# From output 1000 on: convolutions with 13 products per 4 outputs, end terms added onto sums that VectorE seeds in PSUM

## The chip, the cores and the metric

One core of a Trainium2 chip. The metric is the device time of one execution in microseconds (us); lower is better. Times are medians of several executions. On one core an execution counts as slow when it is over 1.5% above the fastest of the same kernel.

Engine names in the profile: PE = TensorE (matmuls), DVE = VectorE, ACT = ScalarE, POOL = GpSimd, SP = SyncE (here: DMA issue).

## The reference, cut to what matters

```python
B, T, D, K, U = 2, 4000, 512, 5, 8
h = gelu(conv5(x, w1))[:, ::2, :]      # 5 taps, zero padding, every second output: 2000 rows per b
f = gelu(conv5(h, w2))[:, ::2, :]      # the same again: 1000 rows per b
fe = f @ w_f;  ge = g @ w_g
j = tanh(fe[:, :, None, :] + ge[:, None, :, :])
out = j @ w_o                          # [2, 1000, 8, 512], bf16
```

So there are two convolutions of stride 2, then a large "joint" product of 16000 rows. The change is to the convolutions. "Output 1000" means row 1000 of `h` for b = 0; the products before it stay as they were, but with tiles of 252 and 248 columns instead of 254 and 246. The joint product is the same, but the PSUM banks that it rotates over are not.

Each kernel's output agreed with the reference within tolerance, but that comparison cannot see the convolutions. Worked out from the reference's inputs on a host, dropping the whole convolution path changes the outputs by less than 1e-6, against a largest output of 2.6e-4. So the runs show times. They do not show that the 13-product arithmetic is right, nor that the end products really accumulate onto what VectorE wrote into PSUM.

## The kernel before: the parts the argument touches

A stride-2 convolution of 5 taps splits into 3 even and 2 odd taps. For 2 outputs at a time, 7 filtered products do the work of 10 direct ones. Each product needs a transformed input (sums and differences of input phases) and a transformed weight.

A tile has 500 column pairs, so each matmul has 500 columns; only the first 1000 outputs are cut into two tiles, t0 and t1, with matmuls of 254 and 246 columns, so that work can start early. One tile is 4 output blocks (`m`) x 7 products x 4 contraction blocks = 112 matmuls.

```python
def xf(src, off, dst, c0, n, which, keep=False):        # VectorE: one transform, 4*n elements
    ...
    elif which == "a1":
        tt("dve", o(1), ph(0), ph(2), add)
    elif which == "a2":
        tt("dve", ph(2), ph(2), ph(0), sub)

def wsum04(wsb, wt, eng, m):                            # GpSimd: weight sums of layer 2
    sl = slice(m * P, (m + 1) * P)
    tt(eng, ssum[:], wsb[0, :, sl], wsb[4, :, sl], add)
    tt(eng, wt[0, :, sl], ssum[:], wsb[2, :, sl], sub)
    tt(eng, wsb[2, :, sl], ssum[:], wsb[2, :, sl], add)

def post(self, m, where, vec=(), scal=(), first=()):    # output transform of one block
    A, C, Dd, step = where
    act(c, ps.cols(C, n), ACT.Copy, scale=0.5)
    ...
    for s, f in ((0, 0.5), (1, -0.5)):                  # VectorE: one input in PSUM
        # t[s] = f * PSUM[Dd] + c
        ...
    for f in vec:                                       # transforms of the next tile
        f()
    tt("dve", tv, tv, ps.pair(A, step, n), add)         # VectorE: SBUF + PSUM
    pending.append(lambda: self.gelu(m, tv))

# entering: the first tiles
t1.xf("a0"); w1sums(0, "s"); w1sums(0, "+"); t1.xf("b1"); t1.xf("b3")
t1.xf("a1"); w1sums(0, "-"); t1.xf("a2"); t1.shift("a3"); t1.xf("a3")
post0(1); post0(2, ...); post0(3)
...
if qi == 3:                                             # late: GpSimd makes layer 2's sums
    wsum13(w2_sb, w2_t, "pool", m * P, (m + 1) * P)
    wsum04(w2_sb, w2_t, "pool", m)
```

Here `tt(engine, out, a, b, op)` is one elementwise operation on two inputs. The layer-1 weight sums are made by VectorE at the start. GpSimd has only small set-up operations until it makes the layer-2 sums from 56 us on. TensorE never needs a result of VectorE *inside* a block: it fills PSUM, and VectorE reads it afterwards.

## Time and profile before

| | before |
|---|---|
| time, median of the first 3 executions | 278.26 us (278.15 to 278.85) |
| span of the profiled execution, granted TensorE clock | 276.5 us, 1.000 |
| TensorE, VectorE, GpSimd busy | 98%, 68%, 11% |
| last matmul group of t1 done, next tile begins | 33.42 us |
| joint product begins | 158.63 us |

The page of the kernel before. The first line after the span has the busy us of each engine, with the share of the span and the number of instructions. The rows after it cut the span into 40 equal slices; each digit is the busy share in tenths (PEclk: the granted clock). The last lines are the chain of work that ended last, by engine.

```profile
span 276.5 us, 3847 instructions
...
PE 271.3 (98%) x1422; PEld 136.7 (49%) x1422; DVE 188.9 (68%) x249; ACT 163.0 (59%) x194; POOL 30.9 (11%) x38
...
PE   8899999999999999999999999999999999999995
...
DVE  2899997977966785775433374766766766766764
...
POOL 1000000079995000000000000000000000000000
PEclk9999999999999999999999999999999999999999
...
PE 96%; DMA 2%; SPq 0%; ACT 0%; issue 0%
```

The chain is TensorE almost alone: a matmul saved anywhere would be time saved. But an average of 68% hides that VectorE is full in slices 3 to 6 (14 to 41 us), exactly where the change adds work.

Lines of the timeline of the kernel before (start us, duration us, engine, line of the program, operation, output<-inputs, shape, count of equal instructions joined):

```profile
22.53 0.67 DVE L287 TENSOR_TENSOR xs<-xs 128x984 bf16<-128x984 bf16 x1
23.11 0.67 DVE L287 TENSOR_TENSOR xt<-xt,xs 128x984 bf16<-128x984 bf16 x1
...
23.66 0.59 PE L298 MATMUL acc<-xs,w_t 128*128 128x246 bf16 x4
24.09 0.58 PE L298 MATMUL acc<-xt,w_sb 128*128 128x246 bf16 x4
...
27.83 1.19 DVE L287 TENSOR_TENSOR xt<-xt,xs 128x2000 bf16<-128x2000 bf16 x1
...
66.49 1.16 POOL L287 TENSOR_TENSOR ssum<-w_sb 128x512 f32<-128x512 bf16 x1
...
66.85 3.93 DVE L287 TENSOR_TENSOR xt<-xt,xs 128x2000 bf16<-128x2000 bf16 x2
70.70 1.18 DVE L287 TENSOR_TENSOR ty<-ty,acc 128x1000 f32<-128x1000 f32 x1
```

Two readings. First, t1's last transform ends at 23.78 us (23.11 + 0.67) and the matmuls that read it start at 24.09: VectorE is 0.3 us ahead of a full TensorE. Second, while GpSimd works at 66 us, a 2000-element transform of two SBUF inputs takes 1.96 us (3.93 for two), instead of the 1.19 us at 27.83 us, where GpSimd is idle. The operation right after it, with one input in PSUM (`acc`), takes its usual 1.18 us.

### The profile page before, as it was taken

What the parts mean: (1) busy time and instruction counts of PE and PEld (TensorE: products, weight loads), DVE (VectorE), ACT (ScalarE), POOL (GpSimd) and SP (SyncE); (2) the same over time, 40 slices, a digit from 0 to 9 for tenths busy, and PEclk for the clock granted to TensorE, in tenths of its full rate; (3) what the DMA queues carried; (4) which work ended last, traced back from release to release, by engine and by line L of the source; (5) the groups of instructions that cost most, each with busy time, mean ns of one, the idle gap of its engine ahead of it and who ended that gap; (6) DMA issues with size and microseconds to landing.
All of it is one profiled execution on the core that took longest, in us unless ns stands there. A gap on an engine that the chain in (4) does not pass through costs nothing.

```text
span 276.5 us, 3847 instructions
## 1 busy us (share of the span) xinstructions
PE 271.3 (98%) x1422; PEld 136.7 (49%) x1422; DVE 188.9 (68%) x249; ACT 163.0 (59%) x194; POOL 30.9 (11%) x38
## 2 busy tenths in 40 slices
PE   8899999999999999999999999999999999999995
PEld 4798844444444444444444444444444444444442
DVE  2899997977966785775433374766766766766764
ACT  2747839357228525624256385849957957966930
POOL 1000000079995000000000000000000000000000
PEclk9999999999999999999999999999999999999999
DMA  7999999992000000000000021444444444444444
GB/s 254 285 165 234 205 194 195 293 322 64 2 0 0 2 0 0 0 2 0 0 1 2 0 76 38 154 152 152 153 154 153 152 154 153 151 150 154 147 149 142
DMA packets 54720, 31.85 MB, mean 115 GB/s; under 512 B 31647, under 2 KB 54447, under 8 KB 54703
## 3 DMA queue, kind: packets, MB, share of 16 engines
q1 hardware_dynamic: 54558, 31.55, 42.4%
q8 instruction: 11, 0.18, 0.3%
q10 hardware_dynamic: 144, 0.07, 0.1%
q14 instruction: 7, 0.05, 0.1%
HBM read 7.86 MB, written 16.38 MB: 88 GB/s over the span
## 4 chain that ended last, share of the span: by engine, by line
PE 96%; DMA 2%; SPq 0%; ACT 0%; issue 0%
PE acc L298 96%; DMA w_sb<-in_w_dram 2%; SPq L322 0%; ACT ost L291 0%
## 5 line engine op out<-in xcount | busy, mean ns | idle before, releaser
L298 PE MATMUL acc<-wo_sb,jT 128*128 128x512 bf16 (+1 forms) x504 | 108.3, 377 | 0.0
L741 DVE CAST ost<-acc 128x512 bf16<-128x512 f32 (+1 forms) x105 | 72.2, 689 | 35.6 <-PE acc L298 35.6
L298 PEld LDWEIGHTS acc<-wo_sb,jT 128*128 128x128 bf16 x504 | 49.3, 98 | 58.8
L298 PE MATMUL acc<-xt,w_sb 128*128 128x500 bf16 (+2 forms) x368 | 76.9, 347 | 0.0
L291 ACT ACTIVATE jT<-feT,geT 128x1000 bf16<-128x1000 f32 (+5 forms) x84 | 70.9, 917 | 0.0
L298 PEld LDWEIGHTS acc<-xt,w_sb 128*128 128x128 bf16 x368 | 36.0, 98 | 31.4
L525 DVE SCALAR_TENSOR_TENSOR ty<-acc,cs 128x500 f32<-128x500 f32 (+2 forms) x54 | 30.4, 605 | 23.1 <-PE acc L298 23.1
L291 ACT ACTIVATE cs<-acc 128x500 f32<-128x500 f32 (+2 forms) x27 | 14.2, 530 | 46.2 <-PE acc L298 46.2
L287 DVE TENSOR_TENSOR ty<-ty,acc 128x1000 f32<-128x1000 f32 (+2 forms) x27 | 28.6, 1058 | 13.6 <-PE acc L298 13.3
L291 ACT ACTIVATE ost<-acc 128x512 bf16<-128x512 f32 (+1 forms) x21 | 12.3, 585 | 31.5 <-PE acc L298 31.5
L298 PE MATMUL acc<-xs,w_t 128*128 128x500 bf16 (+2 forms) x140 | 30.1, 340 | 0.0
L291 ACT ACTIVATE xt<-xs 128x2000 bf16<-128x2000 bf16 (+2 forms) x14 | 21.5, 1567 | 4.7 <-DMA xs<-in_x_dram 4.7
L291 ACT ACTIVATE hT<-ty 128x1000 bf16<-128x1000 f32 (+2 forms) x19 | 18.1, 951 | 6.9 <-DVE ty L287 6.9
L298 PE MATMUL acc<-xs,w_sb 128*128 128x500 bf16 (+2 forms) x104 | 19.4, 318 | 1.0 <-DMA w_sb<-in_w_dram 1.0
L298 PEld LDWEIGHTS acc<-xs,w_t 128*128 128x128 bf16 x140 | 13.5, 97 | 11.2 <-issue 0.4
L298 PE MATMUL acc<-xt,w_t 128*128 128x500 bf16 (+2 forms) x88 | 17.2, 327 | 0.0
L287 DVE TENSOR_TENSOR xt<-xt,xs 128x2000 bf16<-128x2000 bf16 (+2 forms) x14 | 16.0, 1153 | 0.4 <-ACT xt L291 0.3
L298 PE MATMUL acc<-hT,w_t 128*128 128x500 bf16 x64 | 16.1, 374 | 0.0
L298 PE MATMUL acc<-fT,wf_sb 128*128 128x500 bf16 x64 | 13.8, 374 | 0.0
L298 PEld LDWEIGHTS acc<-xs,w_sb 128*128 128x128 bf16 x104 | 10.0, 97 | 7.2 <-DMA w_sb<-in_w_dram 1.2
L291 ACT ACTIVATE fT<-ty 128x1000 bf16<-128x1000 f32 x8 | 10.5, 1315 | 3.6 <-DVE ty L287 3.6
L298 PEld LDWEIGHTS acc<-xt,w_t 128*128 128x128 bf16 x88 | 8.6, 98 | 5.8
(42 smaller groups left out, 133.8 us busy)
## 6 DMA issues: line engine op xcount, KB each, us to landing
out_dram<-ost SPq DMA_DIRECT2D x109, 128.0 KB, 1.9
w_sb<-in_w_dram SPq DMA_DIRECT2D x10, 512.0 KB, 5.6
xr<-in_x_dram SPq DMA_DIRECT2D x2, 512.0 KB, 3.8
wg_sb<-in_w_g_dram SPq DMA_DIRECT2D x1, 512.0 KB, 9.1
wf_sb<-in_w_f_dram SPq DMA_DIRECT2D x1, 512.0 KB, 7.0
wo_sb<-in_w_o_dram SPq DMA_DIRECT2D x1, 512.0 KB, 7.8
xs<-in_x_dram SPq DMA_TRANSPOSE x16, 5.1
out_dram<-ost SPq DMA_DIRECT2D x2, 120.0 KB
```

What stands on the lines that cost most here:

```text
L287: pl.op(eng, lambda e: e.tensor_tensor(out=o.ap, in0=a.ap, in1=b.ap, op=op), (a, b), (o,))
L291: pl.op("act", lambda e: e.activation(o.ap, i.ap, func, scale=scale, bias=0.0 if bias is None else bias.ap), rd, (o,))
L298: ins = e.matmul(o.ap, lhsT=l.ap, rhs=r.ap, start=start and n == 0, stop=stop and n == len(pairs) - 1, skip_group_check=not check)
L525: pl.op("dve", lambda e, o=o, f=f: e.scalar_tensor_tensor(out=o.ap, in0=d.ap, scalar=f, in1=c.ap, op0=ALU.mult, op1=add), (d, c), (o,))
L741: pl.op("dve", lambda e, o=o, v=v: e.tensor_copy(out=o.ap, in_=v.ap), (v,), (o,))
```

## The change

The intent: from output 1000 on, filter over the points 0, 1, -1, infinity and x^2+1, which gives 13 products per 4 outputs instead of 14. Per column the work falls by 1/14; the tiles ("quads") now have 250 columns per matmul.

The two end terms (at 0 and at infinity) belong to single outputs. To save VectorE work they are not added afterwards. VectorE writes its sums of the other products *into PSUM*, and the end products accumulate onto that "seed". So each unit (2 output blocks, 104 matmuls) now has a round trip: TensorE, then VectorE, then TensorE again, while TensorE does the first 32 matmuls (`kq`, `kp`) of the next unit. There are 10 units, u0 to u9: for each of 5 quads two.

The new points need more weight sums. The three of layer 1 that are new come from GpSimd, at the very start (`w1_rest`, 16 operations: per output block one difference and the three sums). The layer-2 sums are 24 operations on GpSimd (20 before) and two on VectorE. The inputs come by 8 transposing loads of 256 rows each, instead of 4 of 512.

The diff, cut to its core (cut: buffers, loads, weight lookup, gelu, banks; lines of dots mark cuts):

```diff
+        def w1_rest(m):
+            sl = slice(m * P, (m + 1) * P)
+            dd = ssum[:]
+            tt("pool", dd, w1_sb[0, :, sl], w1_sb[4, :, sl], sub)
+            tt("pool", w1_t[4, :, sl], dd, w1_sb[2, :, sl], add)
+            tt("pool", w1_t[5, :, sl], dd, w1_sb[2, :, sl], sub)
+            tt("pool", w1_t[1, :, sl], w1_sb[1, :, sl], w1_sb[3, :, sl], sub)
+
+        def w2_even(m, op):
+            ...
+            tt("pool", ssum[:], w2_sb[0, :, sl], w2_sb[4, :, sl], op)
+            tt("pool", w2_a[2 * j, :, sl], ssum[:], w2_sb[2, :, sl], add)
+            tt("pool", w2_a[2 * j + 1, :, sl], ssum[:], w2_sb[2, :, sl], sub)
 ...
+            def xf(self, which):
+                z, r = self.z, self.r
+                if which == "next":
+                    act(r(2), z(0, d=1), ACT.Copy)
+                elif which == "diffs":
+                    tt("dve", r(3, 7), z(4, 8), z(0, 4), sub)
+                elif which == "w":
+                    tt("dve", r(0, 2), r(3, 5), r(5, 7), add)
+                elif which == "d0":
+                    tt("dve", r(2), r(2), z(0), sub)
+                elif which == "sums":
+                    tt("dve", z(0, 4), z(0, 4), z(4, 8), add)
+                elif which == "t+":
+                    tt("dve", z(4, 6), z(2, 4), z(0, 2), add)
+                elif which == "t-":
+                    tt("dve", z(0, 2), z(2, 4), z(0, 2), sub)
+                elif which == "prev":
+                    act(z(2, 4), z(6, 8, d=-1), ACT.Copy)
+                elif which == "d67":
+                    tt("dve", z(2, 4), z(2, 4), z(6, 8), sub)
 ...
+            def unit(self, mp, between=()):
+                ...
+                self.group("kq", mp, bank["kq"])
+                self.group("kp", mp, bank["kp"])
+                finish()                       # end products of the unit before, onto its seed
+                self.group("kw", mp, bank["kw"])
+                self.group("mp", mp, bank["mp"])
+                self.group("mm", mp, bank["mm"])
+                for f in between:              # transforms of the next quad
+                    f()
+                ...
+                act(c2, acc("kw"), ACT.Copy, scale=0.5)
+                stt(sd[2, 0:n], "kq", 0.5, c2, sub)
+                stt(sd[3, 0:n], "kp", 0.5, c2, add)
+                act(c1, acc("mp"), ACT.Copy, scale=0.25)
+                stt(sd[0, 0:n], "mm", 0.25, c1, add)
+                stt(sd[1, 0:n], "mm", -0.25, c1, add)
+                lo, hi = sd[0:2, 0:n], sd[2:4, 0:n]
+                tt("dve", ps.pair(b0 * NT, NT, n), lo, hi, add)     # the seed, into PSUM
+                tt("dve", yy[:, 0:n], lo, hi, sub)
+                ...
+                def end():
+                    self.group("m0", mp, b0, False)
+                    self.group("mi", mp, b3, False)
+                    ...
+                ends.append(end)
 ...
         post0(3)
-        tiles[2].xf("a0")
+        for m in range(NK):
+            w1_rest(m)
 ...
+                if mp == 0:  between = ("next", "diffs", "w", "d0")
+                else:        between = ("sums", "t+", "t-", "prev", "d67")
+                q.unit(mp, [lambda w=w: nx.xf(w) for w in between])
+                if qi == 1 and mp == 0:
+                    for m in range(NK):
+                        w2_even(m, sub)
+                    for m in range(NK):
+                        w2_even(m, add)
+                if qi == 2 and mp == 0:
+                    tt("dve", w2_b[0], w2_sb[1], w2_sb[3], add)
+                    tt("dve", w2_b[1], w2_sb[1], w2_sb[3], sub)
+                    ge()
```

(The `if/else` on `between` is written on two lines here.) In the timelines shown here VectorE and ScalarE run their operations in the order of the program.

## The prediction

> **What bounds the kernel now.** The chain of waits is 96% matmuls; the busy table has TensorE at 98%, VectorE at 68%. In the timeline 246-column matmuls come 105 ns apart, 500-column ones 211 ns: 0.417 ns per column plus 2.5 ns. Weight loads (98 ns) hide under either. But from 20 to 40 us VectorE is 98% busy (table by stage), and its results for the second tile land only 0.3 to 1 us before the matmuls that read them (timelines).
>
> **What the change removes and adds.** Convolution products on whole tiles: 560 matmuls of 500 columns before (118.1 us at 211 ns) become 1040 of 250 (13/14 of the columns, twice the fixed costs; 110.9 us at 106.7 ns). TensorE gain: 7 us, all on the critical path.
>
> VectorE per 1000 outputs, by issue pitch (1.11 us for a 2000-element bf16 or 1000-element fp32 operation, 0.59 us for half): input transforms 6.7 -> 9.3 us, output transforms 9.2 us as before. 18.5 us against 22.2 us of matmuls: sustainable, but each unit's seed must be in PSUM within 3.4 us (the next unit's first 32 matmuls) after its last sum; I count 2.3 us if VectorE is not behind. In every second unit VectorE also waits 2 us for a ScalarE shift; just enough.
>
> **Where it is given back.**
> 1. GpSimd now makes w1 sums: 16 operations of 1.16 us, startable when the w1 loads land (12.9 us). The Trainium skill ("SBUF — State Buffer", section "Who interferes with whom") says that a VectorE instruction with two SBUF inputs contends exclusively with a GpSimd instruction that reads SBUF. This trace agrees: while GpSimd works (56 to 87 us) a 2000-element transform takes up to 1.96 us instead of 1.19, in alternation; operations with one PSUM input stay at 1.19. Before, GpSimd was idle from 13 to 40 us. Now some 15 saturated two-input VectorE operations would alternate with them: up to 0.86 us each, an estimated 8 to 13 us of delay.
> 2. Entering the first 13-product quarter: VectorE has 2.7 us more transforms plus the shift wait, and the first seed is due early: 5 to 7 us of TensorE waiting.
> 3. The w2 sums (24 GpSimd operations, was 20) meet transforms with little slack, and both fp32 sums of SBUF operands, the seed among them: 2 to 5 us.
> 4. First joint products on four rotating banks, not eight: 1 us.
>
> **Prediction.** 278.3 - 7 + (12 + 7 + 4 + 1, shaded down to 18) = 289 us; 8 in 10 between 275 and 301. Chances: over 2% faster 0.14, within 2% 0.20, over 2% slower 0.66.
>
> **What would show it.**
> - Gain: 250-column matmuls 106 to 108 ns apart inside groups, with no idle on weight loads.
> - Step 1: GpSimd busy from 13 to about 37 us; VectorE two-SBUF-input operations of 984 elements at 1.3 to 1.6 us instead of 0.67 there; the second tile's last filtered product starting around 33 to 37 us instead of 24.
> - Step 2: TensorE's first accumulate onto seeded PSUM waiting about 5 us on VectorE.
> - Step 3: seed sums of 1.8 to 2.1 us where GpSimd works on w2; short TensorE waits before end products.
>
> **What would make it wrong.** GpSimd starting later than the w1 landing, or the two engines not alternating on short operations: then step 1 falls to a few us and the result is about 278. If VectorE also reaches the first seed in time, step 2 goes and it is about 272. Worse: idle TensorE could lose clock, or the 8 transposing loads in place of 4 land late.

## The result, and the profile after

| | before | after |
|---|---|---|
| time, median of 4 | 278.2 us (277.76 to 278.85) | 313.77 us (313.25 to 314.74) |
| span and clock of the profiled execution | 276.5 us, 1.000 | 311.5 us, 0.945 |
| TensorE, VectorE, GpSimd busy | 98%, 68%, 11% | 89%, 74%, 23% |

The ratio is 1.127 (95% interval 1.124 to 1.130): slower. A ratio here is always the mean time of one kernel's fast runs over that of the other's of the same rounds, so it is not quite the ratio of the medians that I quote.

The page of the kernel after, the same rows:

```profile
span 311.5 us, 4866 instructions
...
PE 278.2 (89%) x1902; PEld 187.9 (60%) x1902; DVE 229.0 (74%) x256; ACT 163.0 (52%) x209; POOL 71.2 (23%) x58
...
PE   7965599859999299939989899999999999999996
...
DVE  2999999797998999776972707546767676767674
...
POOL 1399900030599998000000000000000000000000
PEclk9997779959999689968999999999999999999999
...
PE 44%; DVE 36%; ACT 10%; issue 9%; DVEq 0%; ACTq 0%
```

The chain of waits is no longer TensorE's: VectorE and ScalarE hold 46% of it. The PE row has holes in slices 3 to 5, 9, 14 and 18 (counting from 1); PEclk falls there or just after.

Lines of the timeline of the kernel after, same columns; a bracket has the engine's idle time just before the instruction and who ended it:

```profile
12.79 2.19 POOL L299 TENSOR_TENSOR ssum<-w_sb 128x512 f32<-128x512 bf16 x1 [5.76 <-DMA w_sb<-in_w_dram]
...
33.60 1.62 DVE L299 TENSOR_TENSOR x<-x 128x992 bf16<-128x992 bf16 x1
35.14 1.62 DVE L299 TENSOR_TENSOR xt<-xt,x 128x992 bf16<-128x992 bf16 x1
...
36.91 0.98 PE L310 MATMUL acc<-xt,w_sb 128*128 128x248 bf16 x4 [1.03 <-DVE xt L299]
...
37.74 1.16 POOL L299 TENSOR_TENSOR w_t<-w_sb 128x512 bf16<-128x512 bf16 x1
...
49.07 3.58 PE L310 MATMUL acc<-xt,w_t 128*128 128x250 bf16 x32
...
50.36 4.71 DVE L299 TENSOR_TENSOR x<-x 128x4000 bf16<-128x4000 bf16 x3
...
57.61 3.58 PE L310 MATMUL acc<-xt,w_t 128*128 128x250 bf16 x32
...
64.69 1.21 DVE L299 TENSOR_TENSOR acc<-sd 128x1000 f32<-128x1000 f32 x1
...
65.99 3.49 PE L310 MATMUL acc<-x,w_sb 128*128 128x250 bf16 x16 [4.81 <-issue]
69.28 3.13 PE L310 MATMUL acc<-xt,w_sb 128*128 128x250 bf16 x24
...
92.60 7.35 DVE L299 TENSOR_TENSOR x<-x 128x4000 bf16<-128x4000 bf16 x3
...
105.52 2.04 DVE L299 TENSOR_TENSOR acc<-sd 128x1000 f32<-128x1000 f32 x1
107.61 3.51 PE L310 MATMUL acc<-x,w_sb 128*128 128x250 bf16 x16 [5.67 <-DVE acc L299]
...
122.78 3.31 DVE L299 TENSOR_TENSOR w_b<-w_sb 128x2048 bf16<-128x2048 bf16 x2
...
137.50 3.51 PE L310 MATMUL acc<-x,w_sb 128*128 128x250 bf16 x16 [5.38 <-DVE acc L299]
...
163.25 1.89 PE L310 MATMUL acc<-hT,w_sb 128*128 128x250 bf16 x16 [1.29 <-DVE acc L299]
```

How to read them:

- **The gain is there.** u0's 80 matmuls of 250 columns run without a gap from 49.07 us to 57.61, where u1 begins: 106.7 ns each, with weight loads hidden. Before, 500-column ones came 210.8 ns apart. 560 x 0.2108 = 118.0 us became 1040 x 0.1067 = 111.0 us: 7.1 us saved before rounding.
- **The entry.** GpSimd starts on the layer-1 weights at 12.79 us, the moment they land, and stops at 38.90. In that stretch the transforms of 992 elements take 1.62 us instead of 0.67. t1's last transform ends at 36.76 us instead of 23.78; its last product starts at 36.91 instead of 24.09.
- **The first seed.** The wait of 4.81 us before 65.99 is put down to "issue". But the seed write (`acc<-sd`) on VectorE ended at 64.69 + 1.21 = 65.90, and those 16 matmuls accumulate onto it. The profile found no semaphore event close enough; the timeline shows who it was.
- **The clock.** The same 16 matmuls take 3.29 us after a wait of 4.81 us (69.28 - 65.99), and 1.73 us after a wait of 1.29 us (the next group starts at 164.98). The Trainium skill ("TensorE: Matmul & The Clock Gate", Part 1) says that the array's clock halves after an idle window of about 3.4 us; these two waits agree. Other waits here do not give so sharp a limit. After a wait of 2.98 us (n_order2) 32 such matmuls took 4.99 us instead of 3.41. Two executions of one kernel, a_fixed, differ: after a wait of 3.59 us 32 matmuls took 5.09 us in one, after 3.57 us only 3.51 us in the other. So half clock followed every wait of 4.8 us and more that is shown here, and only some of those of 2 to 3.6 us.

Where the time went, from the TensorE timeline. The table adds up everything on that line, so its rows also hold half clock. An undisturbed unit is 104 x 0.1067 = 11.10 us (u0 has no end products before it: 8.54 us):

| stretch of TensorE's timeline | us lost | what the trace shows there |
|---|---|---|
| t0 and t1, until the first quad begins (49.07 against 33.42) | 15.65 | 12.82 until t1's last product, then 2.83 at half clock |
| u0 | 0 | 8.54 us |
| u1 | 6.95 | first seed awaited 4.81; then half clock |
| u2, u3 | 0.5 | |
| u4 | 7.45 | seed awaited 5.67; VectorE slowed by GpSimd; half clock |
| u5 | 0.07 | |
| u6 | 7.63 | seed awaited 5.38; two `w_b` sums on VectorE; half clock |
| u7, u8, u9 | 1.5 | seed awaited 1.29 |
| `fe` and start of the joint product | 1.9 | mostly waits, for the copies of `fe` out of PSUM (0.92) and for the first `tanh` (0.70) |
| sum | 41.7 | |

41.7 - 7.1 = 34.6 us, against 35.0 us between the two spans.

### The profile page after: what moved, and what is told of

The parts are those of the page before. It is cut to its first block, busy times and chain, and to the rows that moved or that the text cites. A ratio compares the mean times of both kernels' runs of the same rounds, so it can differ in the third digit from the quotient of the medians.

```text
span 311.5 us, 4866 instructions
## 1 busy us (share of the span) xinstructions
PE 278.2 (89%) x1902; PEld 187.9 (60%) x1902; DVE 229.0 (74%) x256; ACT 163.0 (52%) x209; POOL 71.2 (23%) x58
## 4 chain that ended last, share of the span: by engine, by line
PE 44%; DVE 36%; ACT 10%; issue 9%; DVEq 0%; ACTq 0%
PE acc L310 44%; DVE sd L647 7%; DVE x L299 7%; DVE xt L299 6%; ACT fT L303 4%; DVE yy L299 3%; DVE acc L299 3%; DVE w_t L299 3%; DVE ty L299 3%; ACT jT L303 2%; ACT cc L303 2%; DVE hT L299 1%; DVE ty L532 1%; ACT x L303 1%; DVE w_b L299 1%
## 5 line engine op out<-in xcount | busy, mean ns | idle before, releaser
L310 PE MATMUL acc<-xt,w_sb 128*128 128x250 bf16 (+2 forms) x336 | 42.4, 281 | 4.0 <-DVE xt L299 4.0
L310 PE MATMUL acc<-x,w_sb 128*128 128x250 bf16 (+2 forms) x152 | 24.4, 323 | 17.3 <-DVE acc L299 11.0
L647 DVE SCALAR_TENSOR_TENSOR sd<-acc,cc 128x500 f32<-128x500 f32 x40 | 24.4, 668 | 15.8 <-ACT cc L303 15.6
L299 POOL TENSOR_TENSOR w_a<-ssum,w_sb 128x512 bf16<-128x512 f32 x16 | 28.7, 1815 | 11.9 <-PE acc L310 11.3
L299 POOL TENSOR_TENSOR ssum<-w_sb 128x512 f32<-128x512 bf16 x12 | 23.1, 1922 | 34.5 <-DVE yy L299 28.2
L310 PE MATMUL acc<-xt,w_t 128*128 128x250 bf16 (+2 forms) x232 | 28.7, 281 | 2.5 <-DVE w_t L299 2.5
L310 PEld LDWEIGHTS acc<-x,w_sb 128*128 128x128 bf16 x152 | 16.8, 115 | 23.1 <-DVE acc L299 12.5
L299 DVE TENSOR_TENSOR x<-x 128x2000 bf16<-128x2000 bf16 (+2 forms) x14 | 24.3, 1734 | 6.3 <-ACT x L303 6.1
L310 PE MATMUL acc<-x,w_t 128*128 128x250 bf16 (+1 forms) x208 | 24.3, 273 | 2.3 <-DVE x L299 2.3
L310 PEld LDWEIGHTS acc<-x,w_t 128*128 128x128 bf16 x208 | 20.4, 99 | 4.6 <-DVE x L299 2.6
```

The costliest lines, as they stand in the source:

```text
L299: pl.op(eng, lambda e: e.tensor_tensor(out=o.ap, in0=a.ap, in1=b.ap, op=op), (a, b), (o,))
L310: ins = e.matmul(o.ap, lhsT=l.ap, rhs=r.ap, start=start and n == 0, stop=stop and n == len(pairs) - 1, skip_group_check=not check)
L647: pl.op("dve", lambda e: e.scalar_tensor_tensor(out=o.ap, in0=v.ap, scalar=f, in1=c.ap, op0=ALU.mult, op1=op), (v, c), (o,))
```

## The experiments

Sixteen kernels ran, in four groups; kernels of one group ran on the same chip beside the kernel before, which took 278.17 to 278.57 us (medians) each time. Groups 3 and 4 ran on other chips than groups 1 and 2, so differences across groups are good to about 1 us at best. All had 3 rounds except `h_hybrid` and `h_hybrid2` (5).

The theories:

- **Contention:** GpSimd reading SBUF blocks VectorE operations with two SBUF inputs. The Trainium skill ("SBUF — State Buffer", "Who interferes with whom") says just this: such a VectorE instruction contends with a GpSimd instruction that reads SBUF and not with one that only writes it, and that the lock on the ports they share is exclusive.
- **Order:** even without GpSimd the seed comes late, because VectorE does the next quad's transforms first.
- **Rival A:** half clock after waits is a cost of its own, paid on top.
- **Rival B:** something else of the change is slow: GpSimd being busy at all, late transposing loads, or the matmuls themselves.

### Group 1: is it GpSimd, and is it its reads?

**b_reads16**: the kernel *before*, plus the 16 GpSimd sums, whose results are overwritten before any use.

```diff
 # before.py
         tiles[2].xf("a0")
+        for m in range(NK):
+            sl = slice(m * P, (m + 1) * P)
+            tt("pool", ssum[:], w1_sb[0, :, sl], w1_sb[4, :, sl], sub)
+            tt("pool", w2_t[0, :, sl], ssum[:], w1_sb[2, :, sl], add)
+            tt("pool", w2_t[1, :, sl], ssum[:], w1_sb[2, :, sl], sub)
+            tt("pool", w2_t[0, :, sl], w1_sb[1, :, sl], w1_sb[3, :, sl], sub)
```

> The kernel before, with 16 GpSimd sums over w1 added whose results nobody uses; outputs right. Theory (GpSimd reads alternate with VectorE's two-input operations): about 15 VectorE operations between 13 and 37 us each lengthened by 0.9 us, TensorE delayed by about 14 us, total 290 to 296 us. Rival (the loss is VectorE's own longer queue in the changed kernel, GpSimd harmless): 277 to 281 us.

Measured: **293.81 us**, ratio 1.0565 (1.0526 to 1.0605). Two lines of its timeline on VectorE:

```profile
33.28 1.61 DVE L287 TENSOR_TENSOR xs<-xs 128x984 bf16<-128x984 bf16 x1
34.82 1.62 DVE L287 TENSOR_TENSOR xt<-xt,xs 128x984 bf16<-128x984 bf16 x1
```

These are the same two transforms that stood at 22.53 and 23.11 us before. Sixteen operations added to an idle engine, and nothing else of the change, cost 15.2 us (293.81 - 278.57). That is about the whole entry loss of the kernel after (15.65, half clock included in both).

**a_w1_noread, a_w2_noread, a_noread**: the kernel after, with the layer-1 sums, the layer-2 sums, or both replaced by zero-fills on GpSimd, which write SBUF and read nothing. The weights are then wrong.

```diff
 # after.py; a_w1_noread has the first, a_w2_noread the second, a_noread both
         def w1_rest(m):
-            tt("pool", dd, w1_sb[0, :, sl], w1_sb[4, :, sl], sub)      # and three more
+            for j in (4, 5, 1, 4):
+                memset(w1_t[j])
         def w2_even(m, op):
-            tt("pool", ssum[:], w2_sb[0, :, sl], w2_sb[4, :, sl], op)  # and two more
+            for i in range(3):
+                memset(w2_a[(3 * m + i) % 4])
```

> The changed kernel, the 16 w1 sums on GpSimd replaced by 16 memsets of 2048 elements: GpSimd busy at the same time but reading nothing; outputs wrong on purpose. Theory: VectorE's 984- to 1008-element operations back at 0.67 us, second tile done at about 24 us as before, total 297 to 302 us. Rival (GpSimd being busy is enough, or VectorE's queue is the cause): within 3 us of 313.8.

> The changed kernel, the 24 w2 sums on GpSimd replaced by 24 memsets; outputs wrong on purpose. Theory: the TensorE wait at 102 us (5.7 us and its slow clock) goes, the wait at 132 us shrinks to 2 or 3 us because two VectorE w2 sums still delay that seed; total 299 to 305 us. Rival: within 3 us of 313.8.

> Both replacements together; outputs wrong on purpose. Theory: the two savings add, 283 to 291 us, and what stays above the 271 us of the matmul sum is the first seed, the scalar-shift wait before every second seed and the two VectorE w2 sums. Rival (VectorE's longer queue): 305 us or more.

Measured: **300.8**, **303.46** and **291.41 us** (ratios 1.0803, 1.0895, 1.0461). Against 313.77 these are 13.0, 10.3 and 22.4 us less. Timeline of a_noread, GpSimd and VectorE:

```profile
6.50 28.28 POOL L296 MEMSET w_t<- 128x2048 bf16 x16
...
22.71 0.67 DVE L299 TENSOR_TENSOR x<-x 128x992 bf16<-128x992 bf16 x1
23.29 0.67 DVE L299 TENSOR_TENSOR xt<-xt,x 128x992 bf16<-128x992 bf16 x1
```

GpSimd is busy without a gap from 6.50 to 34.78 us, and VectorE runs at full speed beside it. So "GpSimd busy" (one reading of rival B) falls, and the reads are it. The skill's rule holds in both halves: reading costs 0.95 us per VectorE operation, only writing costs nothing. The zero-fills had one artefact: the first quad's first product waited 1.1 us for a small one that stood behind them.

But a_noread is still 13 us slower than before, 20 us above 278.2 - 7.1. Its first seed was still awaited for 5.07 us. That wait is what the order theory is about. a_w2_noread shows what the layer-2 reads did to the later waits. They were 5.67 us (in u4) and 5.38 us (in u6); without the reads they are these:

```profile
103.30 1.88 PE L310 MATMUL acc<-x,w_sb 128*128 128x250 bf16 x16 [0.55 <-DVE acc L299]
...
128.47 2.71 PE L310 MATMUL acc<-x,w_sb 128*128 128x250 bf16 x16 [2.41 <-DVE acc L299]
```

### Group 2: order, place, clock

**a_order, a_noread_order**: my first reordering. The transforms go behind the seed; `prev` (a ScalarE copy) comes last in its unit, and `d67` moves into the next unit.

```diff
 # after.py (a_order) and a_noread (a_noread_order)
-                for f in between:
-                    f()
                 act(c2, acc("kw"), ACT.Copy, scale=0.5)
                 stt(sd[2, 0:n], "kq", 0.5, c2, sub)
                 stt(sd[3, 0:n], "kp", 0.5, c2, add)
+                for f in mid:                       # ("d67",) of this quad, when mp == 0
+                    f()
 ...
                 tt("dve", yy[:, 0:n], lo, hi, sub)
+                for f in post:                      # transforms of the next quad
+                    f()
-                    between = ("next", "diffs", "w", "d0")
-                    between = ("sums", "t+", "t-", "prev", "d67")
+                    post = ("next", "diffs", "w", "d0", "sums")
+                    post = ("t+", "t-", "prev")
```

> The changed kernel with VectorE's input transforms for the next quarter moved behind the seed of each unit (same instructions, same GpSimd work). If the order of VectorE's queue is a cause of its own, the wait before the first seeded accumulate (5 us and its slow clock) falls to about 1 us and the later ones shrink: 294 to 303 us. If only GpSimd's reads cost: within 4 us of 313.8.

> The same order, and both GpSimd sums as memsets (outputs wrong on purpose). If contention and order are together the whole loss beside a few us, this comes near the 271 us of the matmul sum: 275 to 281 us. If the seeding or the banks cost something of their own: still above 285.

Measured: **317.45** (fast executions alone: 317.42) and **292.59 us**. Both were misses: no gain at all, against 294 to 303 and 275 to 281 expected. Both numbers fall where the expectation put its rival (only the reads cost; the seeding costs something itself). The timeline of a_noread_order, VectorE and ScalarE, says why:

```profile
65.01 2.44 DVE L299 TENSOR_TENSOR x<-x 128x2000 bf16<-128x2000 bf16 x2
72.11 1.26 DVE L638 SCALAR_TENSOR_TENSOR sd<-acc,cc 128x500 f32<-128x500 f32 x2 [4.67 <-ACT cc L303]
...
67.61 1.89 ACT L303 ACTIVATE x<-x 128x2000 bf16<-128x2000 bf16 x1 [7.24 <-DVE x L299]
69.40 1.18 ACT L303 ACTIVATE hT<-yy 128x500 bf16<-128x500 f32 x2
...
71.42 1.06 ACT L303 ACTIVATE cc<-acc 128x500 f32<-128x500 f32 x2
```

The shift `prev` (`x<-x` on ScalarE) waits for VectorE's `t-`. It stood in ScalarE's queue ahead of gelus and of the `cc` copies that VectorE's sums need. ScalarE idled 7.24 us with work behind it, and then VectorE idled 4.67 us. So the edit made a new wait, and the order theory was neither shown nor refuted by these two; n_order2 below removes that wait.

**a_late**: the first GpSimd sum is held back until t1's last transform is done.

```diff
-            tt("pool", dd, w1_sb[0, :, sl], w1_sb[4, :, sl], sub)
+            a, b, hold = w1_sb[0, :, sl], w1_sb[4, :, sl], t1.a[2][2]     # hold: t1's "a3" result
+            pl.op("pool", lambda e: e.tensor_tensor(out=dd.ap, in0=a.ap, in1=b.ap, op=sub), (a, b, hold), (dd,))
```

> The changed kernel, outputs right, its first GpSimd w1 sum held until VectorE has finished the second tile's last transform. Theory: the second tile's products run as before (done near 24 us), but the sums now meet the first quarter's transforms, which gives back about a third: 299 to 308 us. Rival (holding does not help, the same contention moves along unchanged): within 3 us of 313.8.

Measured: **305.32 us** (1.0982), in the range. t1's last product is back at 24.44 us. The contention moved to the first quad's transforms (three of them took 6.44 us together, against 4.71 in the kernel after), and the first seed was still awaited, 5.30 us. In this place too the sums met VectorE's two-input work; no other place was tried.

**a_warm** tests rival A. In each of the three long waits TensorE gets 40 filler matmuls on data at hand, into a bank that the next product restarts. They keep TensorE busy while it would wait.

```diff
+                if (self.layer, self.b, self.half, mp) in ((1, 0, 1, 1), (1, 1, 1, 0), (2, 0, 0, 0)):
+                    for _ in range(5):
+                        for i in range(2):
+                            self.product("kw", ev, 2 * mp + i, bank["kw"] * NT + i * NQ, i == 0)
                 finish()
```

> The changed kernel with 40 idle matmuls (4.3 us) put into each of the three waits of 5 to 6 us before seeded accumulates. If TensorE loses clock in those waits and that costs 2 us each, the total falls by 4.5 to 6 us, to 308 to 309.5. If the slow matmuls are hidden by other waits: unchanged or slightly slower, 313 to 315.

Measured: **312.19 us**, ratio 1.1233 (1.1186 to 1.128): 1.6 us less than 313.77, not the 4.5 to 6 expected, and not clear of the noise (the kernel after has 1.124 to 1.130). TensorE's timeline:

```profile
60.72 4.43 PE L310 MATMUL acc<-xt,w_sb 128*128 128x250 bf16 x40
65.97 1.87 PE L310 MATMUL acc<-x,w_sb 128*128 128x250 bf16 x16 [0.81 <-issue]
...
79.48 1.88 PE L310 MATMUL acc<-x,w_sb 128*128 128x250 bf16 x16 [2.26 <-DVE acc L299]
```

The clock was kept: 16 matmuls are back to 1.70 us (67.67 - 65.97). But TensorE then arrived early at the *next* seed and waited 2.26 us there. VectorE sets the pace in these stretches. The half clock, 5.8 us on TensorE's timeline in u1, u4 and u6, mostly hid behind VectorE, and rival A is worth at most a few us there (1.6 measured, within the noise). (The 2.83 us in t1 were not tested this way.)

### Group 3: order done right, and sums on VectorE

**n_order2**: no sums on GpSimd (seven zero-fills in their place; wrong weights), and a better order. `prev` stands behind the `c2` copy of the next unit, `d67` behind the seed.

```diff
                 act(c2, acc("kw"), ACT.Copy, scale=0.5)
+                if own:                              # mp == 0: this quad's own shift
+                    self.xf("prev")
 ...
                 tt("dve", ps.pair(b0 * NT, NT, n), lo, hi, add)
+                if own:
+                    self.xf("d67")
                 tt("dve", yy[:, 0:n], lo, hi, sub)
+                for f in post:
+                    f()
-                    between = ("next", "diffs", "w", "d0")
-                    between = ("sums", "t+", "t-", "prev", "d67")
+                    post = ("next", "diffs", "w", "d0")
+                    post = ("sums", "t+", "t-")
```

> No GpSimd sums (a few memsets, outputs wrong on purpose), VectorE's transforms behind the seed, and now ScalarE's shift behind the copy that the next seed needs, so that neither in-order queue blocks a seed. If the two queues' order is the rest of the loss: TensorE's wait before the first seeded accumulate under 1 us instead of 5, none above 1 us later, 275 to 281 us. If VectorE simply has too much work: 286 us or more.

Measured: **284.26 us** (1.0198), 3 us above the range and below the rival's 286 ("too much work"). TensorE's timeline:

```profile
43.01 5.15 PE L310 MATMUL acc<-x,w_t 128*128 128x250 bf16 x32 [2.98 <-issue]
...
51.91 1.87 PE L310 MATMUL acc<-x,w_sb 128*128 128x250 bf16 x16 [0.34 <-issue]
...
63.00 1.87 PE L310 MATMUL acc<-x,w_sb 128*128 128x250 bf16 x16
```

The order theory holds: the first seed is awaited 0.34 us instead of 5.07 (a_noread), the second not at all. So a seed written by VectorE need not hold TensorE up by more than 0.34 us. What stayed was the entry (2.98 us before 43.01, then half clock) and 4.1 us at `fe`, where the new order left VectorE's copies late (a wait of 2.28 us, then half clock).

**a_dvesums, a_fixed, h_hybrid** have the sums right, all on VectorE, as operations of 2048 bf16 elements (1.22 us each; 12 in all, where the kernel after had 2 on VectorE). a_dvesums keeps the order of the kernel after; a_fixed has that of n_order2; h_hybrid is a_fixed with the second half of layer 1's b = 0 left at 7 products, so that the sums need not be ready so early.

```diff
-        for m in range(NK):
-            w1_rest(m)
+        tt("dve", w1_t[5], w1_sb[0], w1_sb[4], sub)
+        tt("dve", w1_t[4], w1_t[5], w1_sb[2], add)
+        tt("dve", w1_t[5], w1_t[5], w1_sb[2], sub)
+        tt("dve", w1_t[1], w1_sb[1], w1_sb[3], sub)
 # and eight for layer 2, two after each unit of quads 1 and 2, w2_b among the last four
```

> The changed kernel in its own order, but all weight sums on VectorE as ten 2048-element bf16 operations (1.1 us each) in place of 40 on GpSimd. If contention is what the GpSimd sums cost, 11 us more of VectorE work is cheaper than they were: 294 to 303 us, against 313.8. Rival (VectorE's load is the cost, wherever it comes from): 313 us or more.

> The sums on VectorE and the order of n_order2: a whole 13-product kernel without contention. Entering the first quarter VectorE is still 4 to 6 us behind, so 279 to 286 us: about as slow as before or slightly slower, not the 271 of the matmul sum.

> As a_fixed, but the first batch's second half keeps its 7 products per 2 outputs, so that VectorE meets the 13-product form one quarter later: the matmul sum is 272.6 us. If being behind at the entry is what is left, this is the fastest: 273 to 279 us. If not: 280 or more.

Measured: **302.93** (in the range), **296.25** and **297.17 us** (fast executions alone: 296.39; both far above). In a_fixed one wait makes most of the miss: I had put a `w2_b` sum behind the transforms, too late for its first reader. TensorE's timeline of a_fixed:

```profile
117.30 1.01 PE L310 MATMUL acc<-xt,w_b 128*128 128x250 bf16 x4 [7.78 <-DVE w_b L299]
```

h_hybrid has its `w2_b` sums in the same late place. In the profile of a fast execution, the same wait is 9.62 us.

### Group 4: what is left over

**a_order2** is the kernel after with the order of n_order2 and its GpSimd sums kept. **n_order3** is n_order2 with the copies of the first `fe` all on ScalarE. **a_fixed2** and **h_hybrid2** are a_fixed and h_hybrid with that and with the `w2_b` sums earlier.

```diff
 # n_order3, a_fixed2, h_hybrid2
-                    if m % 2:
+                    if m % 2 or b == 0:
                         act(o, v, ACT.Copy)
```

> The changed kernel with its GpSimd sums, in the order of n_order2 (transforms behind seeds on VectorE, the shift behind the needed copy on ScalarE). If order and contention add: 7 us less than 313.8, 304 to 309 us. If VectorE is so loaded by contention that order does not matter: 311 to 317.

> n_order2 (outputs wrong on purpose) with the eight copies of the first joint products all on ScalarE, behind nothing of VectorE. If those products waited on VectorE's queue, the 4 us there go: 279 to 281.5 us; what is left is the entry into the first quarter, 6 us. Otherwise 283 to 285.

> a_fixed with its w2 sums placed before they are needed and the copies of n_order3. The wait of 8 us on a w2 sum and its slow clock go: 280 to 286 us, still above before because of 4 to 8 us at the entry.

> h_hybrid with the same two repairs: four of five quarters in the 13-product form, entered when VectorE is no longer behind. Matmul sum 272.6 us; 273.5 to 279 us. If it stays above 281, the entry is not what is left.

Measured: **305.26** (fast executions alone: 304.96), **279.33** (1.004), **285.31** (1.0255) and **283.58 us** (1.0185). The first three are in their ranges. The last is 4.6 us above its own, and above the 281 at which its expectation gave up the entry as the rest of the loss in that kernel.

a_order2 completes a table of two by two (medians of fast executions; the right column is from groups 3 and 4):

| us | order of the change | seed first |
|---|---|---|
| GpSimd sums | 313.77 | 304.96 |
| zero-fills instead | 291.41 | 284.26 |

The sums' contention is worth 22.4 or 20.7 us, the order 8.8 or 7.2. Within 2 us they add up: two separate causes. (The zero-fills are 40 on the left and seven on the right.) Together they do not explain all: 284.26 us is still 13 us above 278.2 - 7.1.

n_order3 takes 4.9 of these 13 us away. It is the fastest version of this change that I measured, with wrong weights and the GpSimd sums free, and it only equals the kernel before. Nearly all of its 7.1 us of saved matmuls go to the entry. Its first quad starts at 35.11 us (33.42 before) and u0 takes 13.44 us (8.54). One line of VectorE's timeline in n_order3:

```profile
32.81 2.24 DVE L299 TENSOR_TENSOR xt<-x 128x4000 bf16<-128x4000 bf16 x1 [2.35 <-DMA x<-in_x_dram]
```

VectorE waits 2.35 us for the transposed inputs of the first quad, and the quad's other transforms follow from there. So rival B's loads play a part, but only once contention is gone. In the kernel after VectorE was too late to notice them. Whether 4 loads of 512 rows would have landed earlier was not tested.

In a_fixed2 and h_hybrid2 the sums are on VectorE and the weights right in intent. h_hybrid2 waits 2.33 us at its first quad for a weight sum that I placed last, and 2.07 us for a later seed, with half clock after each. **No version beat the kernel before.** A better placing might gain those few us; that stays open.

## Why the prediction was wrong

The direction was right (slower, at 0.66), and every step named was found in the trace. Of its checks in the profile most came true: GpSimd busy from 12.79 to 38.90 us ("13 to about 37"), transforms at 1.62 us ("1.3 to 1.6"), t1's last product at 36.91 us ("33 to 37"), the first seed awaited 4.81 us ("about 5"), contended seeds at 2.04 us ("1.8 to 2.1"). One did not: the "short TensorE waits" of step 3 were 5.67 and 5.38 us. The sum came out at 313.77 us, above the range of 275 to 301. The terms of the sum, as the prediction put them:

| term | predicted | measured | |
|---|---|---|---|
| gain on matmuls | 7 | 7.1 | right: 106.7 ns apart |
| 1. w1 sums on GpSimd against two-input operations | 12 | 15.65 (alone on the kernel before: 15.2) | right mechanism; VectorE's delay was 13.0, the top of "8 to 13"; half clock added 2.8 |
| 2. first seed | 7 | 6.95 | right in size, in part by luck: 4.81 is the wait, just under "5 to 7", and the rest half clock; the wait stays at 5.07 without GpSimd and falls to 0.34 in the new order |
| 3. w2 sums; "2 to 5 us" | 4 | u4 7.45, u6 7.63 | too small by a factor of almost four |
| 4. `fe` on four banks | 1 | 1.1 | right in size; that the number of banks is the reason was not tested |
| "shaded down to 18" | -6 | 0 | wrong: no overlap is seen |

**The step that failed is "12 + 7 + 4 + 1, shaded down to 18".** Two parts of it were wrong. The losses came to 41.7 us, 23.7 more than 18: 6 are the shading, 11.1 term 3, 3.7 term 1, and 2.9 small losses that no term had.

1. *The shading.* I took 6 us off in case the steps hid behind each other. They lie one after the other on TensorE's line (until 49 us, at 61, at 102, at 132 us), with full TensorE work between them. The unshaded sum would have given 295 us. The two-by-two table shows the same for contention and order: within 2 us they add.
2. *Term 3.* I counted it as "little slack" and did not add up VectorE's line between two seeds. Between 88.58 and 107.56 us VectorE has six contended operations: the seed and `yy` of u2 (2.04 and 2.14 us instead of 1.21 and 1.19), three transforms (7.35 instead of 4.71), the seed of u3 (2.04 instead of 1.21). That is 5.25 us more, and TensorE, in u4, waited 5.67 us for that last seed. The prediction's own figure, up to 0.86 us for each, gives 5.2 us for these six: the number was there, the count was not made. In u6 I had overlooked the two `w2_b` sums on VectorE, which stand in the diff. They took 3.31 us right behind a seed, and the wait was 5.38 us. Taking GpSimd's w2 reads away recovered 10.3 us, more than twice the term. The wait in u4 fell to 0.55 us and the one in u6 to 2.41, so the rest of u6 is VectorE's own queue. The 1.29 us before 163.25 stayed (1.27), so it is no part of term 3.

The prediction named lost clock as a risk without a number. It shows on TensorE's timeline as 2.8 us in t1 and 5.8 us in the units. But a_warm recovered only 1.6 us of the latter, within the noise, so it was not the main miss.

What stays open: how much of t1's 2.8 us of half clock would come back with a warm TensorE; whether a placing of the sums on VectorE exists that beats 278 us; what share of the entry is the late loads and what VectorE's longer transforms; what the slow executions were. Whether the 13-product outputs are right numerically was not tested, as the comparison cannot see them.

## What to carry to other kernels

An idle engine was not free here: before work is moved to GpSimd, look at what VectorE does in the same stretch. Count its operations with two SBUF inputs, and multiply by what a contended one costs in the same trace. When a result goes TensorE, VectorE, TensorE, add up the whole in-order queue that stands before it on *each* engine between two such hand-overs, put the hand-over first in it, and check that nothing in that queue waits for something slow. And don't shade a sum of delays that lie at different times on the critical engine: here they added.

## What the Trainium skill lacked or had wrong

- "SBUF — State Buffer", section "Who interferes with whom": right in both halves here. It names two ratios (VectorE 6.8 times, GpSimd 1.5 times slower) without the operations, and no duration for two streams of short operations that contend for long. Measured: 0.67 us becomes 1.62 us for each 992-element bf16 operation beside GpSimd operations of 512 elements (1.16 us alone, mostly 1.6 beside VectorE), over 24 us; 16 such GpSimd operations cost this kernel 15.2 us (b_reads16). GpSimd zero-fills without a gap for 28 us cost nothing: 0.67 us stayed.
- "TensorE: Matmul & The Clock Gate", Part 1: the half rate after waits is confirmed (16 matmuls of 250 columns in 3.29 us after a wait of 4.81 us, 1.73 us after 1.29 us). Its limit, one idle window of about 3.4 us, is too long for these runs: half rate came after shorter waits too (2.98 us in n_order2: 32 matmuls in 4.99 us instead of 3.41; 2.33 us in h_hybrid2: 12 in 2.09 us instead of 1.28). It lacks that the loss can be nearly free when another engine sets the pace: keeping the clock in three such waits gave 1.6 us of 5.8, within the noise.
- "PSUM — Partial Sum Buffer", "The four PSUM rules", rule 2, says that only TensorE changes the bits that make a matmul accumulate or overwrite. It has no time for an fp32 sum written into PSUM as a seed: a write of 1000 fp32 elements into PSUM took 1.21 us, the same as into SBUF (1.19 us), and with a good order TensorE waited at most 0.34 us for the first seeds (n_order2).
- No page explains single executions that take 1.5 to 3.1 times as long as the others of the same kernel (581.04 against 296 us, 472.08 against 305 us at a clock of 0.559, 994.94 against 317 us). "TensorE: Matmul & The Clock Gate" has only a warning of a clock seen stuck low; whether that is the 472.08 us was not looked into.
